# Sparse attention and a mixture of experts on one Trainium2 core: source order in place of scheduled order for the expert part

## The chip, the core and the metric

The kernel runs on one core of one Trainium2 chip. The core has five engines that run their own instruction queues side by side and meet only at semaphores: TensorE for matmuls (PE in the rows, PEld for its weight loads), VectorE (DVE), ScalarE (ACT), GpSimd (POOL) and SyncE, whose queue (SPq) issues the transfers. The metric is the device time of one execution in microseconds, as the median of several runs.

## The reference

Two steps follow each other. The first is block-sparse attention over 4 batches, 8 heads, 768 positions and 64 dimensions per head. The second takes its output as 3072 rows of 512 numbers, gives each row a weight for each of 8 experts by repeated normalisation of rows and columns, and adds up eight two-layer networks:

```python
attn = softmax(where(mask, q @ k.T / sqrt(64), -1e9)) @ v       # [4, 8, 768, 64]
x = attn.transpose(0, 2, 1, 3).reshape(3072, 512)
P = exp(x @ w_gate - max)                                        # [3072, 8]
for _ in range(8):
    P /= P.sum(1) + 1e-9;  P /= P.sum(0) + 1e-9;  P *= 3072 / 8
for e in range(8):
    out += P[:, e:e+1] * (maximum(x @ w1[e], 0) @ w2[e])         # w1[e] 512x1024, w2[e] 1024x512
```

## The kernel before, in words

The attention fills the first 470 us or so and is written out by a table of due times; its instructions are chained one behind the other on each engine, in the order in which they are written. It also brings the first expert's weights in and stores x, split into pieces, in DRAM.

The change is in the expert part that follows. Work goes by `i = 4 e + b`, expert `e` and batch `b` (`B` is 4). Both layers are done by a seven-product scheme on 2x2 blocks: products numbered 0, 1, 5, 6, 3, 4, 2 in the order of use, each of its own combination of blocks. Since every operand is a pair of half-precision numbers (a high and a low part), a product is three matmuls per slice of the contraction.

- **Stage one**, `stage1(i, qi)`: for each of four quarters of half the hidden width, the seven products of x with the first layer's weights. One product is six matmuls of 384 columns into one of four PSUM banks (`p`). Behind each product VectorE folds the bank into the tiles `a1`, `r11`, `u3`, `c21` ("combs", line 1145), ScalarE applies the relu, GpSimd forms the sums that the second stage wants (lines 1207 and 1033). Each of the seven results becomes a pair `h`: a high half on ScalarE (line 1155) and a low half on VectorE or GpSimd (lines 1159 and 1165).
- **Stage two**, `stage2(i, p)`: for product p three groups of twelve matmuls of 256 columns into one of four banks (`py`, line 1248), and behind each group VectorE adds the bank into the output tile `acc` (line 1269).
- **Weights.** The next expert's raw weights come into a single buffer `r` by one transfer of 2 MB (line 173): first `w1`, and once it is used up `w2`. `scale_w` finds their largest number (eight reductions `mx`, line 187, then a few small steps, one of them on TensorE) and from it a power of two. GpSimd forms the differences of blocks that the scheme needs (`queue_sum`, line 1026). Seven splits (`queue_split`) then write the pairs: the high part on ScalarE (line 1011), the low part on VectorE (line 1015). The pairs of w1 lie in the tiles `arena` and `attic` and those of w2 in `w2p`. There is one set of each, so a split has to wait until the old product's last matmul is done.

Four quarters of the next batch alternate with the stage-two products of this one: products 0 and 1, quarter 0, product 5, quarter 1, products 6 and 3, quarter 2, products 4 and 2, quarter 3.

Small steps are put between them by `Slots`, a planner that runs while the kernel is built: each step carries a delay in ticks (one tick per product or group) and costs for VectorE, ScalarE and GpSimd, and it is written into the program when its delay is over and the planner's account of that engine is not ahead of TensorE's. Steps added as `lazy` (weights) come after the urgent ones, in the order in which they were added. What `Slots` writes is the source order. In the kernel before, the framework's own scheduler then orders the instructions of the expert part again on each engine, by a timeline that it estimates itself; only the attention part is chained.

## Time and profile before

| what | value |
|---|---|
| median of 3 runs | 2358.24 us (2353.56 to 2359.13) |
| profiled execution, its own time | 2357.4 us |
| its span | 2355.6 us |
| TensorE busy | 2200.1 us, 93% |
| VectorE busy | 2014.4 us, 86% |
| ScalarE, GpSimd busy | 1256.0 us, 1287.1 us |

The profile is of one execution. Its page gives the busy time of each engine, the span in slices, the chain of work that ended last, and the costliest groups of instructions by source line. The trace behind it can be asked for windows (busy time of each engine in a stretch), for the instructions of a tile or a line, for waits, and for a timeline. A row of a timeline gives start and length in microseconds, engine, line, operation, output and input, and in brackets the idle time before it with what ended that.

### The profile page before, as it was taken

To read this page: it belongs to the slowest core of one execution; us is meant where nothing else is said; L and a number is where in the kernel's file an instruction comes from. 1 tells how busy PE (TensorE), PEld (TensorE's weight loads), DVE (VectorE), ACT (ScalarE), POOL (GpSimd) and SP (SyncE) were. 2 spreads that over 40 slices of the span, in tenths; PEclk is the share of its full clock that TensorE was granted. 3 is DMA by queue.
4 is the path that set the end of the run, shared out by engine and by line. 5 is a ranking of instruction groups with operands and counts; after the bars stand their busy time and mean duration, and the time that the engine had idled before them with its cause. 6 is when DMAs were issued, how large, how long until landed. Compare 5 with 4: busy or idle time off the path is not lost.

```text
span 2355.6 us, 47334 instructions
## 1 busy us (share of the span) xinstructions
PE 2200.1 (93%) x18892; PEld 1608.6 (68%) x18892; DVE 2014.4 (86%) x3570; ACT 1256.0 (53%) x2173; POOL 1287.1 (55%) x1235
## 2 busy tenths in 40 slices
PE   5999998879999999999989999999899999998999
PEld 3766666647666677677667776776677667766777
DVE  8999999888789878987898789878987898789876
ACT  4888878655465445444444445444544454445442
POOL 2012334496367645765576557655865486548543
PEclk9999999999999999999999999999999999999999
DMA  6667765422121212121212121212211221121221
GB/s 152 135 123 151 186 131 121 135 97 75 48 82 50 83 48 83 48 83 48 83 48 83 48 84 52 80 48 83 64 68 48 84 80 52 48 84 48 75 75 54
DMA packets 191888, 192.34 MB, mean 82 GB/s; under 512 B 131740, under 2 KB 144052, under 8 KB 191668
## 3 DMA queue, kind: packets, MB, share of 16 engines
q1 hardware_dynamic: 191104, 189.30, 28.2%
q8 instruction: 147, 2.41, 0.4%
q14 instruction: 73, 0.60, 0.1%
q10 hardware_dynamic: 564, 0.03, 0.0%
HBM read 140.54 MB, written 17.30 MB: 67 GB/s over the span
## 4 chain that ended last, share of the span: by engine, by line
PE 57%; DVE 21%; POOL 9%; issue 6%; DMA 4%; ACT 3%; SPq 0%; DVEq 0%; POOLq 0%; ACTq 0%
PE py L1248 25%; PE p L1135 23%; POOL r L1026 3%; DVE top L673 3%; DMA r<-in_moe_w_dram 3%; DVE h L1165 2%; PE u L731 2%; POOL h L1165 2%; DVE u L1145 2%; DVE acc L1269 2%; DVE mx_w L187 2%; PE t L697 1%; PE m L664 1%; PE t L700 1%; PE m L667 1%
## 5 line engine op out<-in xcount | busy, mean ns | idle before, releaser
L1248 PE MATMUL py<-w2p,h 128*128 128x256 f16 x8064 | 971.1, 275 | 52.7 <-ACT h L1155 23.7
L1248 PEld LDWEIGHTS <-h 128*128 128x128 f16 x8064 | 790.1, 99 | 209.9 <-ACT h L1155 28.8
L1269 DVE SCALAR_TENSOR_TENSOR acc<-py,spare,acc 128x256 f32<-128x256 f32 (+1 forms) x840 | 459.2, 581 | 49.5 <-PE py L1248 46.9
L1165 POOL TENSOR_TENSOR h<-u,h 128x384 f16<-128x384 f32 x128 | 127.0, 992 | 601.3 <-ACT h L1155 601.3
L1135 PEld LDWEIGHTS <-attic 128*128 128x128 f16 x3072 | 301.8, 98 | 195.9 <-issue 22.5
L1135 PE MATMUL p<-attic 128*128 128x384 f16 x2304 | 413.2, 328 | 16.4 <-DVE r L1145 14.4
L1135 PE MATMUL p<-arena 128*128 128x384 f16 x2304 | 407.6, 327 | 19.4 <-DVE a L1145 11.2
L1135 PEld LDWEIGHTS <-arena 128*128 128x128 f16 x2304 | 225.9, 98 | 153.5 <-issue 24.8
L1155 ACT ACTIVATE h<-c 128x384 f16<-128x384 f32 x256 | 133.6, 522 | 330.7 <-DVE c L1145 256.7
L705 ACT ACTIVATE pe<-t,shift,qk 128x768 int32<-128x768 f32 x192 | 189.7, 989 | 78.6 <-PE t L700 73.0
L1145 DVE SCALAR_TENSOR_TENSOR a<-p,a 128x384 f32<-128x384 f32 x384 | 211.1, 550 | 18.9 <-PE p L1135 14.3
L673 DVE TENSOR_REDUCE top<-m 128x1 f32<-128x768 f32 x192 | 181.8, 949 | 16.7 <-PE m L667 16.4
L1155 ACT ACTIVATE h<-r 128x384 f16<-128x384 f32 x256 | 132.5, 521 | 66.5 <-POOL r L1033 63.0
L1207 POOL TENSOR_TENSOR s<-a,u 128x384 f32<-128x384 f32 x128 | 129.6, 1013 | 68.7 <-ACT a L1204 68.7
L1033 POOL TENSOR_TENSOR r<-s,r 128x384 f32<-128x384 f32 x128 | 155.4, 1214 | 9.6
L1033 POOL TENSOR_TENSOR c<-c,r 128x384 f32<-128x384 f32 x128 | 150.8, 1178 | 10.0
L1135 PE MATMUL p<-arena,attic 128*128 128x384 f16 x768 | 146.1, 327 | 0.0
L1026 POOL TENSOR_TENSOR r<-r 128x256 f32<-128x256 f32 (+1 forms) x106 | 135.0, 1290 | 20.0 <-DVE arena L1015 17.9
L664 PE MATMUL m<-kt,qt 128*128 128x512 f16 (+1 forms) x384 | 129.6, 338 | 14.5 <-DVE top L673 7.2
L1165 POOL TENSOR_TENSOR h<-r,h 128x384 f16<-128x384 f32 x128 | 142.8, 1115 | 0.2 <-ACT h L1155 0.2
L1145 DVE SCALAR_TENSOR_TENSOR r<-p,a 128x384 f32<-128x384 f32 x128 | 70.7, 552 | 79.0 <-PE p L1135 59.4
L697 PE MATMUL t<-qt,kt 128*128 128x512 f16 (+1 forms) x384 | 127.9, 333 | 10.8 <-DVE top L673 10.6
(206 smaller groups left out, 3683.1 us busy)
## 6 DMA issues: line engine op xcount, KB each, us to landing
arena<-xd SPq DMA_DIRECT2D x128, 384.0 KB, 3.9
attic<-xd SPq DMA_DIRECT2D x96, 384.0 KB, 3.9
r<-in_moe_w_dram SPq DMA_DIRECT2D x16, 2048.0 KB, 8.4
arena<-in_q_dram SPq DMA_DIRECT2D x16, 384.0 KB, 4.5
arena<-in_k_dram SPq DMA_DIRECT2D x16, 384.0 KB, 4.8
arena<-in_v_dram SPq DMA_DIRECT2D x4, 1536.0 KB, 8.5
xd<-xs_t SPq DMA_DIRECT2D x16, 384.0 KB, 4.6
out_dram<-acc SPq DMA_DIRECT2D x24, 256.0 KB, 2.0
```

Source lines behind the costliest of these rows:

```text
L664: nc.tensor.matmul(sc[:, lo:hi], lhsT=qt[:, 0, c], rhs=ka[:, lo:hi], start=True, stop=False)
L673: nc.vector.tensor_reduce(out=tops[n][:, c : c + 1], in_=sc[:, :S], axis=AX.X, op=ALU.max)
L697: nc.tensor.matmul(sc[:, lo:hi], lhsT=kt[:, 0, c], rhs=qa[:, lo:hi], start=True, stop=False)
L705: nc.scalar.activation(pe, sc[:, :S], AF.Exp, bias=shift, scale=qk[n // 2][3])
L1026: lambda c=c: Pinned.gpsimd.tensor_tensor(out=out[:, c], in0=x[:, c], in1=y[:, c], op=op),
L1033: nc.gpsimd.tensor_tensor(out=out, in0=x, in1=y, op=ALU.subtract)
L1135: nc.tensor.matmul(ps, lhsT=w1p[p][:, l, kc, fs], rhs=xp[p][:, r, kc], start=(kc == 0 and m == 0), stop=(kc == KH - 1 and m == 2),)
L1145: nc.vector.scalar_tensor_tensor(out=t, in0=ps, scalar=HDOWN, in1=other, op0=ALU.mult, op1=ALU.add)
L1155: nc.scalar.activation(h[:, 0], src, AF.Relu if relu else AF.Copy)
L1165: eng.tensor_tensor(out=h[:, 1], in0=src, in1=h[:, 0], op=ALU.subtract)
L1248: nc.tensor.matmul(py, lhsT=hs[i, p, kc][:, l, tsl], rhs=w2p[p][:, r, kc], start=(kc == 0 and m == 0), stop=(kc == KF // 2 - 1 and m == 2),)
L1269: nc.vector.scalar_tensor_tensor(out=dst, in0=src, scalar=c, in1=dst, op0=ALU.mult, op1=ALU.add)
```

## The change

Three things are done at once.

1. Every instruction of the expert part is tied to the one written before it on the same engine (`hold_from(held)` at the end), so that each engine runs in source order. The tie is of a kind that adds no semaphore (`NoSync`): it only binds the scheduler.
2. The splits of the next `w1` are no longer all added at the start of the expert's last batch. They are added inside the last quarter of stage one with the old weights, each behind the old weight's last product (`used`), and taken in another order (6 before 5). `load_w(2, ...)` and `scale_w(2, ...)` stand ahead of quarter 0 and no longer behind it.
3. The differences of `w2` blocks are formed in another way (through `t1`, eight of the sixteen pieces before the scale is known), and its splits come later: 0 and 1 after product 5, 6 and 5 after products 6 and 3, the other three after products 4 and 2.

Some costs and delays of the planner differ too. Only the core of the diff is shown.

```diff
+        def hold_from(n):
+            for ins in traced[n:]:
                 if ins.engine in newest:
                     tc.add_manual_dep(
                         ins, newest[ins.engine], behind, reason="keep_in_program_order"
                     )
                 newest[ins.engine] = ins.name
...
         xlast = finish_x(B - 1)
+        held = len(traced)
...
-            slots.add(part, key, 6 if k == 0 else 1, True, dve=0.6)
+            slots.add(part, key, 8 if k == 0 else 1, True, dve=0.65)
...
-            key, delay, True, act=1.04,
+            key, delay, True, act=1.1,
...
-            key, delay + 1, True, dve=1.2,
+            key, 1, True, dve=1.4,
...
-                key, 1, True, pool=2.4 / n,
+                key, 1, True, pool=3.2 / n,
...
+        def first():
+            one(0, a[0, 0])
+            queue_sum(a[0, 0], a[1, 0], a[0, 0], ("w1", e, 5))
+        def second():
+            one(1, a[0, 1])
+            queue_sum(a[0, 1], a[0, 1], a[0, 0], ("w1", e, 2))
+        def third():
+            one(6, s3)
+            one(5, a[0, 0])
+        return {
+            0: first, 1: second, 6: third,
+            3: lambda: one(3, a[1, 1]), 4: lambda: one(4, a[1, 0]), 2: lambda: one(2, a[0, 1]),
+        }
...
+        def sums():
+            queue_sum(t1, m[0, 1], m[0, 0], ("scale", 2, e))
+            queue_sum(m[0, 1], m[0, 1], m[1, 1], ("scale", 2, e))
+        def first():
+            one(0, m[0, 0])
+            queue_sum(m[0, 0], m[1, 1], t1, ("w2", e, 5))
+            one(1, m[1, 0])
+            queue_sum(m[1, 0], m[1, 0], m[0, 0], ("w2", e, 3))
         return [
-            lambda: one(5, t2),
-            lambda: (one(6, m[0, 1]), one(3, m[1, 0])),
-            lambda: (one(4, m[0, 0]), one(2, m[1, 1])),
+            sums,
+            first,
+            lambda: (one(6, m[0, 1]), one(5, m[0, 0])),
+            lambda: (one(4, t1), one(3, m[1, 0]), one(2, m[1, 1])),
         ]
...
+            if used and p in used:
+                used[p]()
...
-                stage1(i + 1, qi)
+                swap = qi == FH // P - 1 and b == B - 2 and nxt
+                stage1(i + 1, qi, split_w1(e + 1) if swap else None)
...
-        if last:
-            split_w1(e + 1)
         stage2(i, 0)
         stage2(i, 1)
-        quarter(0)
         if last:
...
             load_w(2, e + 1)
-            if not PRE:
-                scale_w(2, e + 1)
+            parts = split_w2(e + 1, wr[2])
+            scale_w(2, e + 1)
+            parts[0]()
             queue_weight(e + 1)
-            parts = split_w2(e + 1, wr[2])
+        quarter(0)
         stage2(i, 5)
         if last:
-            parts[0]()
+            parts[1]()
...
+    hold_from(held)
```

What it moves is best seen in the queues. The names say the batch and the quarter: `p5_15_3` is product 5 of batch 15, quarter 3, and `py_15_1_2` is the third group of stage-two product 1. Batch 15 is the last of expert 3, so the weights that change here are those of expert 4. Lines from 1017 on stand a little lower in the changed file: 1015 has become 1021, 1145 has become 1165, 1165 has become 1185, 1269 has become 1289, 1011 has become 1017.

VectorE before, in the last quarter with expert 3's weights:

```order
L1145 SCALAR_TENSOR_TENSOR r11_15_3_18694<-p1_15_3_18695,a1_15_3_18685 128x384
L1015 SCALAR_TENSOR_TENSOR arena_92<-r1_4_17448,sw1_4_17452,arena_92 128x1024
L1145 SCALAR_TENSOR_TENSOR a1_15_3_18685<-p5_15_3_18706,a1_15_3_18685 128x384
L1015 SCALAR_TENSOR_TENSOR attic_96<-s3_4_17454,sw1_4_17452,attic_96 128x1024
L1145 SCALAR_TENSOR_TENSOR u3_15_3_18714<-p6_15_3_18715,a1_15_3_18685 128x384
L1165 TENSOR_TENSOR h_5_8094<-r11_15_3_18694,h_5_8094 128x384
L1015 SCALAR_TENSOR_TENSOR attic_96<-r1_4_17448,sw1_4_17452,attic_96 128x1024
L1145 SCALAR_TENSOR_TENSOR c21_15_3_18723<-p3_15_3_18724,u3_15_3_18714 128x384
L1015 SCALAR_TENSOR_TENSOR arena_92<-r1_4_17448,sw1_4_17452,arena_92 128x1024
L1015 SCALAR_TENSOR_TENSOR attic_96<-r1_4_17448,sw1_4_17452,attic_96 128x1024
L1145 SCALAR_TENSOR_TENSOR u3_15_3_18714<-p4_15_3_18734,u3_15_3_18714 128x384
```

The same place now, and then the end of the stage-two products 0 and 1 behind it:

```order
L1021 SCALAR_TENSOR_TENSOR arena_92<-r1_4_17448,sw1_4_17452,arena_92 128x1024
L1165 SCALAR_TENSOR_TENSOR r11_15_3_18698<-p1_15_3_18699,a1_15_3_18685 128x384
L1185 TENSOR_TENSOR h_5_8094<-r11_15_3_18698,h_5_8094 128x384
L1021 SCALAR_TENSOR_TENSOR arena_92<-r1_4_17448,sw1_4_17452,arena_92 128x1024
L1165 SCALAR_TENSOR_TENSOR a1_15_3_18685<-p5_15_3_18712,a1_15_3_18685 128x384
L1165 SCALAR_TENSOR_TENSOR u3_15_3_18721<-p6_15_3_18722,a1_15_3_18685 128x384
L1021 SCALAR_TENSOR_TENSOR attic_96<-s3_4_17454,sw1_4_17452,attic_96 128x1024
L1165 SCALAR_TENSOR_TENSOR c21_15_3_18734<-p3_15_3_18735,u3_15_3_18721 128x384
L1165 SCALAR_TENSOR_TENSOR u3_15_3_18721<-p4_15_3_18744,u3_15_3_18721 128x384
```

```order
L1185 TENSOR_TENSOR h_25_8114<-a1_15_3_18685,h_25_8114 128x384
L1021 SCALAR_TENSOR_TENSOR arena_92<-r1_4_17448,sw1_4_17452,arena_92 128x1024
L1289 SCALAR_TENSOR_TENSOR acc_3_10006<-py_15_1_2_18862,spare_6_16716,acc_3_10006 128x256
L1021 SCALAR_TENSOR_TENSOR attic_96<-r1_4_17448,sw1_4_17452,attic_96 128x1024 x3
L1165 SCALAR_TENSOR_TENSOR r11_16_0_18897<-p1_16_0_18898,a1_16_0_18888 128x384
L1165 SCALAR_TENSOR_TENSOR a1_16_0_18888<-p5_16_0_18908,a1_16_0_18888 128x384
```

Before, all seven splits stand within that one quarter, ahead of its last combs; now three stand in the quarter and four behind the stage-two groups that follow it. The low half `h_5`, which needs ScalarE's answer to the comb of `r11`, had two combs and two splits between it and that comb; now it comes right behind.

VectorE before, at the splits of w2:

```order
L1015 SCALAR_TENSOR_TENSOR w2p_0_8082<-r2_4_18957,sw2_4_18961,w2p_0_8082 128x1024
L1269 SCALAR_TENSOR_TENSOR acc_3_10006<-py_15_2_2_19374,spare_6_16608,acc_3_10006 128x256
L1015 SCALAR_TENSOR_TENSOR w2p_1_8083<-r2_4_18957,sw2_4_18961,w2p_1_8083 128x1024
L1165 TENSOR_TENSOR h_25_8114<-s1_16_2_19266,h_25_8114 128x384
L1165 TENSOR_TENSOR h_20_8109<-a1_16_2_19190,h_20_8109 128x384
L1015 SCALAR_TENSOR_TENSOR w2p_2_8084<-r2_4_18957,sw2_4_18961,w2p_2_8084 128x1024
L1145 SCALAR_TENSOR_TENSOR r11_16_3_19400<-p1_16_3_19401,a1_16_3_19390 128x384
L1145 SCALAR_TENSOR_TENSOR a1_16_3_19390<-p5_16_3_19414,a1_16_3_19390 128x384
L1015 SCALAR_TENSOR_TENSOR w2p_4_8086<-r2_4_18957,sw2_4_18961,w2p_4_8086 128x1024
```

VectorE now:

```order
L1021 SCALAR_TENSOR_TENSOR w2p_0_8082<-r2_4_18881,sw2_4_18886,w2p_0_8082 128x1024
L1165 SCALAR_TENSOR_TENSOR a1_16_3_19379<-p5_16_3_19410,a1_16_3_19379 128x384
L1165 SCALAR_TENSOR_TENSOR u3_16_3_19419<-p6_16_3_19420,a1_16_3_19379 128x384
L1165 SCALAR_TENSOR_TENSOR c21_16_3_19430<-p3_16_3_19431,u3_16_3_19419 128x384
L1179 SCALAR_TENSOR_TENSOR h_19_8108<-c21_16_3_19430,h_19_8108 128x384
L1021 SCALAR_TENSOR_TENSOR w2p_1_8083<-r2_4_18881,sw2_4_18886,w2p_1_8083 128x1024
L1165 SCALAR_TENSOR_TENSOR u3_16_3_19419<-p4_16_3_19444,u3_16_3_19419 128x384
```

Four splits within nine rows have become two within seven; the other five now come after stage-two product 1 of batch 16 and later.

ScalarE at the start of the expert part, before (batch 0, quarter 1):

```order
L1155 ACTIVATE h_4_8093<-a1_0_0_8121 128x384
L769 ACTIVATE xf_3_6824<-u_0_144 128x384
L1011 ACTIVATE w2p_0_8082<-r2_0_7728,sw2_0_7732 128x1024
L1011 ACTIVATE w2p_1_8083<-r2_0_7728,sw2_0_7732 128x1024
L1011 ACTIVATE w2p_2_8084<-r2_0_7728,sw2_0_7732 128x1024
L1155 ACTIVATE h_7_8096<-r11_0_1_8209 128x384
```

And now (batch 0, the end of quarter 3):

```order
L1224 ACTIVATE a1_0_3_8362<-a1_0_3_8362 128x384
L1017 ACTIVATE w2p_0_8082<-r2_0_7728,sw2_0_7732 128x1024
L1286 ACTIVATE acc_0_8119<-py_0_0_0_8465 128x512 x2
L1286 ACTIVATE acc_0_8119<-py_0_0_1_8480 128x512 x2
L1286 ACTIVATE acc_0_8119<-py_0_0_2_8495 128x512 x2
L1017 ACTIVATE w2p_1_8083<-r2_0_7728,sw2_0_7732 128x1024
```

The first expert's w2 splits have moved from the second quarter of the first batch to behind its last. On TensorE the first product of the expert part now stands behind the attention's last matmul, and no group of matmuls is cut up by another any more.

36 lines of the change are left out of this document (11 added, 25 removed).

## The prediction

> **What bounds the kernel now.** I read the page first, then windows one expert long, then the moments in which TensorE waits.
>
> ```profile
> span 2355.6 us, 47334 instructions
> PE 2200.1 (93%) x18892; PEld 1608.6 (68%) x18892; DVE 2014.4 (86%) x3570; ACT 1256.0 (53%) x2173; POOL 1287.1 (55%) x1235
> ```
>
> Two engines are near full. In the chain of waits (start, length, what) the load of each expert's w2 marks a period, and the long pieces give TensorE's own pace:
>
> ```profile
> 699.22 9.23 DMA r<-in_moe_w_dram
> 931.79 8.52 DMA r<-in_moe_w_dram
> 1361.32 7.32 PE py L1248 x67
> 1368.63 3.90 PE p L1135 x24
> 2101.10 8.50 DMA r<-in_moe_w_dram
> ```
>
> Five periods take 2101.10 - 931.79, so one takes 233.9 us. Unhindered, a product of stage one is 3.90/4 = 0.975 and a stage-two group 12 x 7.32/67 = 1.31. An expert has 4 x 4 x 7 products (109.2) and 4 x 7 x 3 groups (110.1): 219.3 us. So 14.6 us of each period are lost. The windows of one period (length; busy time of PE, PEld, DVE, ACT, POOL; clock) say where:
>
> ```profile
> 931.80:1165.80 234.00, 224.26 (x1682) 164.95 (x1682) 199.00 (x344) 110.03 (x206) 145.43 (x137) 0.99 0.20 66
> 1145.00:1185.00 40.00, 35.18 (x267) 25.53 (x265) 35.12 (x53) 17.02 (x27) 18.89 (x16) 1.00 0.39 122
> 1210.00:1240.00 30.00, 24.27 (x169) 16.27 (x167) 27.78 (x35) 15.67 (x26) 29.61 (x28) 0.96 0.36 115
> 1240.00:1385.00 145.00, 144.47 (x1106) 108.35 (x1105) 116.57 (x215) 65.59 (x130) 84.20 (x82) 1.00 0.14 49
> ```
>
> For 145 us TensorE never stops, with VectorE at 80%. It stops where the weights change: at w1's splits (1145 to 1185) and at w2's (1210 to 1240), with VectorE at 88 and 93% and GpSimd full in the second. Its waits there, and VectorE's queue:
>
> ```profile
> 1164.65 1.14 PE L1135 MATMUL p<-arena 128*128 128x384 f16 x6 [1.66 <-DVE a L1145]
> 1237.93 3.53 PE L1248 MATMUL py<-w2p,h 128*128 128x256 f16 x17 [3.21 <-ACT h L1155]
> 1158.52 2.28 DVE L1015 SCALAR_TENSOR_TENSOR attic<-r,sw,attic 128x1024 f16<-128x1024 f32 x1
> 1161.19 1.27 DVE L1015 SCALAR_TENSOR_TENSOR arena<-r,sw,arena 128x1024 f16<-128x1024 f32 x1
> 1163.58 0.55 DVE L1145 SCALAR_TENSOR_TENSOR u<-p,u 128x384 f32<-128x384 f32 x1
> 1164.05 0.54 DVE L1145 SCALAR_TENSOR_TENSOR a<-p,a 128x384 f32<-128x384 f32 x1
> 1165.71 2.72 DVE L1269 SCALAR_TENSOR_TENSOR acc<-py,spare,acc 128x512 f32<-128x512 f32 x4
> 1170.59 1.26 DVE L1269 SCALAR_TENSOR_TENSOR acc<-py,spare,acc 128x256 f32<-128x256 f32 x3
> ```
>
> A split takes 1.27 to 2.28; the combs that free the banks queue behind seven of them.
>
> **The change, part by part.** It adds no work: seven splits, eight reductions and the sums stay. What counts is when VectorE gets them. A comb costs 0.47 (1163.58 to 1164.05), a wide acc 0.67, a narrow one 0.41. The rest come from the groups (busy, mean ns), less 0.08 which overlaps with the next:
>
> ```profile
> L1165 DVE TENSOR_TENSOR h<-a,h 128x384 f16<-128x384 f32 x128 | 127.4, 995 | 0.3 <-ACT h L1155 0.3
> L1165 DVE TENSOR_TENSOR h<-s,h 128x384 f16<-128x384 f32 x128 | 106.8, 834 | 27.3 <-ACT h L1155 27.1
> L1165 DVE TENSOR_TENSOR h<-r,h 128x384 f16<-128x384 f32 x128 | 97.3, 760 | 15.0 <-ACT h L1155 14.8
> L1159 DVE SCALAR_TENSOR_TENSOR h<-c,h 128x384 f16<-128x384 f32 x128 | 78.6, 614 | 2.4 <-ACT h L1155 2.4
> L187 DVE TENSOR_REDUCE mx_w<-r 128x1 f32<-128x512 f32 x128 | 79.1, 673 | 16.1 <-DMA r<-in_moe_w_dram 16.1
> L1015 DVE SCALAR_TENSOR_TENSOR attic<-r,sw,attic 128x1024 f16<-128x1024 f32 x21 | 33.8, 1608 | 0.0
> ```
>
> So low halves 0.91, 0.75, 0.68, 0.53, a reduction 0.59, a split 1.53. A quarter is 7 combs and two low halves: 4.5 against TensorE's 6.8. Counting the new queue piece by piece at the change of expert (VectorE against TensorE): the last old quarter with three splits, one of them ahead of its first comb, 9.1 against 6.8, less 1.5 done while the groups before it (which leave 2.7 free) run: +0.8; product 0, +0.1; product 1 with four splits and two low halves 9.0 against 3.9: +5.1. VectorE is then 6.0 behind. TensorE has four banks, so it runs three products (2.9) ahead: **3.1 us lost** at the new quarter 0. Then the spare time of quarters (2.3 each) pays the rest off; the eight reductions add 4.8 over quarter 1 and three products, and leave VectorE under 1 behind. A second hump stands at the next batch: two splits in quarter 3 (+1.1), two behind product 1 (+2.1), one each in quarter 0 (-0.8) and behind product 5 (+2.4): 4.8, **1.9 us lost**. I take 5 per change of expert. Bounds: nothing lost (0), and as now (14.6).
>
> Covered: the load of w2 is issued behind the last split, lands 8.5 later, and its first reduction stands 6.8 + 3.9 + 3.9 = 14.6 behind; if it came late, VectorE would stop and every comb behind it. SyncE has the seven x loads ahead of it, as now. The regrouped differences are sixteen pieces as before, eight of them ahead of the scale. With quarters 13.7 apart on average and GpSimd at 145.4/16 = 9.1 per quarter, they find room. The ties cost nothing by themselves; the price is that an engine no longer steps around a wait.
>
> That price falls due at the **start**, where the scheduler had mixed attention, batch 0, the last x pieces and w2's splits:
>
> ```profile
> 462.20:572.80 110.60, 95.36 (x744) 65.50 (x742) 94.06 (x153) 59.18 (x113) 81.77 (x73) 0.97 0.23 80
> 463.40 0.55 DVE L716 TENSOR_SCALAR pl<-pe 128x768 f16<-128x768 uint16 x1
> 475.97 3.22 ACT L1011 ACTIVATE w2p<-r,sw 128x1024 f16<-128x1024 f32 x3
> 501.73 2.08 PE L1135 MATMUL p<-arena 128*128 128x384 f16 x6 [5.72 <-DVE c L1145]
> 504.03 2.12 PE L1135 MATMUL p<-arena 128*128 128x384 f16 x6
> ```
>
> In 110.6 us eight quarters and 21 groups were done (82.1), so some 25 were lost, after the attention's rest. Now the first product waits for the attention's last weights (463.40) and what hangs on them: about 467 instead of 462.2, 4.5 later. The splits of w2, which ScalarE did at 476, come behind quarter 3, one by one between the copies of the output: following the queue with 1.07 (3.22 for three) for a high half and 1.27 to 1.53 for a low one I get waits of about 6.6, 3.6 and 7.3 ahead of products 0, 1 and 5. The last x pieces, now within product 2, cost about 7 in two waits for splits, and small waits 5. That is 30 lost plus 4.5, against 25: +10. After waits this long matmuls run at half pace for a while (2.08 and 2.12 for six, where 1.14 is usual): two such waits for one, +2. I take **+12**; bounds -20 (all lost time goes, but the later start stays) and +30 (the x pieces' chain costs twice, the balance steps stop TensorE too).
>
> Sum: 2355.6 - 7 x (14.6 - 5) + 12 = 2300.4 of span. The profiled execution took 2357.4, 1.8 more than its span, and the median is 0.8 above it: **2303 us**.
>
> **Rivals.** *Splits at the slow price.* Now w1's first splits stand next to GpSimd's sums, and by order the last three wait on ScalarE behind halves that GpSimd's chain feeds. At 2.28 each (1158.52) seven splits put 5.3 more on VectorE, 10 lost instead of 5: 2303 + 35 = 2338. Against it: 1.27 occurs as well. The Trainium skill (SBUF — State Buffer, Who interferes with whom) says that a VectorE instruction with two SBUF inputs shuts out, or is shut out by, a GpSimd one that reads SBUF. The trace agrees: combs, with one input there, stay at 0.55, splits spread. By that rule alone, always losing, it would be this rival.
>
> *All of it goes.* TensorE never stops at a change and the start costs what it did: 2358 - 102 = 2256. For it: 145 us without a stop. Against: 6.0 behind is more than four banks cover.
>
> *VectorE becomes the bound.* In order, it stops where the low half of r11 comes right behind its comb. What that takes stands here:
>
> ```profile
> 1198.88 0.56 DVE L1145 SCALAR_TENSOR_TENSOR r<-p,a 128x384 f32<-128x384 f32 x1 [0.25 <-ACT a L1180]
> 1199.98 0.51 ACT L1184 ACTIVATE r<-r 128x384 f32<-128x384 f32 x1
> 1200.52 0.52 ACT L1155 ACTIVATE h<-r 128x384 f16<-128x384 f32 x1
> ```
>
> From 1199.44 to 1201.04: 1.6, and some 0.6 for c21. VectorE's 199.0 per period plus 16 quarters x 2.2 is 234: the point from which it is slower. At 2.5 a quarter it is 239 for each of eight experts: 2358 + 8 x 5.1 + 12 = 2411. Against it: the low half comes right behind only where the planner counts VectorE as free, and in the 145 us it has 28 to spare, 2.7 a quarter. The Trainium skill (TensorE: Matmul & The Clock Gate, Architectural detail) calls VectorE's and ScalarE's queues strict FIFO, which is what makes such a stop total; it changes none of these numbers.
>
> *Nothing to see.* The same work on a VectorE as full as before: the waits only move, and the start eats the rest: 2358.
>
> **Chances.** Forecast 0.55, slow splits 0.18, all of it 0.14, VectorE bound 0.09, nothing 0.04. A difference under 0.3% can't be told from none. Faster: 0.55 + 0.18 + 0.14 = 0.87; same 0.04; slower 0.09. The range runs from between "all of it" and the forecast to "slow splits": 2266 to 2340; 0.04 + 0.09 and about half of 0.14 lie outside.
>
> **What would show it.** Right: period near 224, the windows at w1's and w2's splits at 95% for TensorE, three splits within the last old quarter, TensorE's longest waits of a period at new quarter 0 for DVE r; w2's load issued about 22 after the last old quarter begins; waits over 5 us only between 495 and 570. Wrong: waits for combs in batches without weight work (VectorE bound), a first reduction that waits for the DMA, a period over 229 with splits near 2.2, or an expert part that reaches the second w2 load (699.22 now) much earlier or later than 711 less 5 to 10.

## The result and the profile after

The changed kernel takes **2467.7 us** (median of 4 runs, 2458.15 to 2477.5) where the kernel before takes 2357.37 beside it: a ratio of 1.0471, 95% interval 1.0427 to 1.0514. It is slower by 110 us; 2303 was forecast. The profile after is of the fastest of the four executions (2458.15), so it accounts for 100.8 of the 110 us. In the text below "lead" is the distance that TensorE can run ahead of VectorE because four PSUM banks hold its products, and a "stop" is time in which an engine stands in front of an instruction whose input isn't there.

The head of the page after:

```profile
span 2456.4 us, 47436 instructions
PE 2206.7 (90%) x18892; PEld 1611.4 (66%) x18892; DVE 1995.6 (81%) x3570; ACT 1270.8 (52%) x2173; POOL 1255.0 (51%) x1235
```

The work is the same, and the busy times hardly differ (TensorE 2200.1 then, 2206.7 now; VectorE 2014.4 then, 1995.6 now). Of the 100.8 us of span, 94 are idle time of TensorE. The issues of SyncE's weight loads say where (start, length; w2 of experts 1, 2 and 7):

```profile
743.74 0.38 SPq L173 DMA_DIRECT2D r<-in_moe_w_dram  x1
...
989.78 0.38 SPq L173 DMA_DIRECT2D r<-in_moe_w_dram  x1
...
2203.53 0.38 SPq L173 DMA_DIRECT2D r<-in_moe_w_dram  x1
```

The first mark is 44.5 later than before (699.22). The last five periods take (2203.53 - 989.78)/5 = 242.8 instead of 233.9, and the one ahead of them 246.0 instead of 232.6: 57.9 in all. Behind the last mark 1.6 are won. So there are two losses: about 44 at the start and about 9 in each period of 243.

One period in windows (length; busy time of PE, PEld, DVE, ACT, POOL; clock): the whole, the stretch behind the w2 load, the clear middle, and the last old quarter with what follows it up to the next load:

```profile
1476.10:1718.40 242.30, 222.13 (x1682) 164.14 (x1682) 197.12 (x344) 111.83 (x206) 141.12 (x136) 1.00 0.19 64
1476.10:1561.50 85.40, 74.25 (x561) 54.63 (x561) 75.19 (x127) 41.13 (x74) 53.16 (x53) 1.00 0.18 58
1561.50:1694.20 132.70, 129.56 (x990) 96.59 (x989) 100.19 (x190) 57.42 (x114) 74.46 (x73) 1.00 0.17 59
1694.20:1718.40 24.20, 18.32 (x135) 12.92 (x133) 21.74 (x28) 13.27 (x19) 13.50 (x11) 1.00 0.34 114
```

TensorE idles for 20.2 of 242.3: 11.2 behind the load, 3.1 in the middle, 5.9 in the last old quarter. So 17 of 20 are still lost where the weights change, in 110 us. VectorE works 96.9 of these 110.

What is new is VectorE's own idle time. Its longest waits over the whole run (engine, line and tile, what ended them: us in all, times, longest), first after, then the row of before that answers to the first (c21's halves, at L1159 then, had 2.4):

```profile
DVE h L1185 <- ACT h L1175: 172.0, 174, 1.2
...
DVE h L1179 <- ACT h L1175: 53.6, 91, 0.6
```

```profile
DVE h L1165 <- ACT h L1155: 42.3, 104, 1.9
```

VectorE stands in front of low halves, waiting for ScalarE's high halves, for 225.6 us. At r11's it waits about 1.1 in 93 of the 128 quarters, those in which the half stands right behind its comb, and at c21's 0.6 in 91. The remaining 61 us are at s1's halves, which had 27 before. The waits at r11 and c21 are the stop of the third rival. TensorE's waits after:

```profile
PE p L1153 <- DVE a L1165: 54.0, 44, 2.7
PE p L1153 <- DVE r L1165: 43.4, 28, 3.1
PE all_w L110 <- DVE ma_w L193: 23.6, 14, 2.9
```

The third is new as well: in order, TensorE stands in front of the transpose that spreads a weight's maximum until VectorE has reduced it.

VectorE's queue and TensorE's at the last old quarter (start, length, instruction, in brackets the idle time ahead of it):

```profile
1695.20 1.28 DVE L1021 SCALAR_TENSOR_TENSOR arena<-r,sw,arena 128x1024 f16<-128x1024 f32 x1 [2.05 <-ACT arena L1017]
1696.40 0.55 DVE L1165 SCALAR_TENSOR_TENSOR r<-p,a 128x384 f32<-128x384 f32 x1
1698.09 1.38 DVE L1185 TENSOR_TENSOR h<-r,h 128x384 f16<-128x384 f32 x1 [1.15 <-ACT h L1175]
1699.40 1.27 DVE L1021 SCALAR_TENSOR_TENSOR arena<-r,sw,arena 128x1024 f16<-128x1024 f32 x1
1700.59 0.55 DVE L1165 SCALAR_TENSOR_TENSOR a<-p,a 128x384 f32<-128x384 f32 x1
```

```profile
1701.19 1.14 PE L1153 MATMUL p<-attic 128*128 128x384 f16 x6 [2.72 <-DVE a L1165]
1714.38 0.82 PE L1153 MATMUL p<-arena 128*128 128x384 f16 x4 [1.91 <-DVE arena L1021]
```

A split stands ahead of the first comb and waits 2.05 for ScalarE; then the low half waits 1.15; then the next split; and the comb of product 5, which would free a bank, ends at 1701.14. TensorE waits 2.72 for it.

### The profile page after: what moved, and what is told of

Read it like the earlier page. It is cut to its first block, busy times and chain, and to the rows that moved or that the text cites. A ratio compares the mean times of both kernels' runs of the same rounds, so it can differ in the third digit from the quotient of the medians.

```text
span 2456.4 us, 47436 instructions
## 1 busy us (share of the span) xinstructions
PE 2206.7 (90%) x18892; PEld 1611.4 (66%) x18892; DVE 1995.6 (81%) x3570; ACT 1270.8 (52%) x2173; POOL 1255.0 (51%) x1235
## 4 chain that ended last, share of the span: by engine, by line
PE 53%; DVE 32%; ACT 6%; issue 5%; DMA 2%; POOL 1%; SPq 0%; DVEq 0%; POOLq 0%
PE py L1268 26%; PE p L1153 20%; DVE acc L1289 5%; DVE h L1185 4%; DVE a L1165 3%; DVE top L673 3%; DVE w2p L1021 3%; ACT h L1175 2%; DVE u L1165 2%; PE u L731 2%; DVE mx_w L187 2%; DVE r L1165 1%; PE m L664 1%; PE t L697 1%; PE m L667 1%
## 5 line engine op out<-in xcount | busy, mean ns | idle before, releaser
L1268 PE MATMUL py<-w2p,h 128*128 128x256 f16 x8064 | 917.9, 275 | 27.9 <-ACT w2p L1017 14.2
L1185 POOL TENSOR_TENSOR h<-u,h 128x384 f16<-128x384 f32 x128 | 131.9, 1030 | 766.0 <-ACT h L1175 766.0
L1289 DVE SCALAR_TENSOR_TENSOR acc<-py,spare,acc 128x256 f32<-128x256 f32 (+1 forms) x840 | 447.2, 581 | 19.1 <-PE py L1268 11.5
L1153 PE MATMUL p<-arena 128*128 128x384 f16 x2304 | 400.7, 328 | 9.4 <-DVE arena L1021 7.4
L1185 DVE TENSOR_TENSOR h<-r,h 128x384 f16<-128x384 f32 x128 | 87.3, 682 | 111.0 <-ACT h L1175 110.8
L1185 DVE TENSOR_TENSOR h<-s,h 128x384 f16<-128x384 f32 x128 | 118.1, 923 | 60.9 <-ACT h L1175 60.8
L1204 ACT ACTIVATE r<-r 128x384 f32<-128x384 f32 x128 | 66.9, 523 | 188.3 <-DVE r L1165 188.3
L1039 POOL TENSOR_TENSOR c<-c,r 128x384 f32<-128x384 f32 x128 | 142.8, 1115 | 28.0 <-ACT c L1232 18.1
L1039 POOL TENSOR_TENSOR r<-s,r 128x384 f32<-128x384 f32 x128 | 146.5, 1145 | 10.0
L1185 POOL TENSOR_TENSOR h<-r,h 128x384 f16<-128x384 f32 x128 | 138.3, 1081 | 4.8 <-ACT h L1175 4.8
L1032 POOL TENSOR_TENSOR r<-r 128x256 f32<-128x256 f32 (+1 forms) x106 | 122.5, 1181 | 28.6 <-DVE arena L1021 28.6
```

The costliest lines, as they stand in the source:

```text
L1032: lambda c=c: Pinned.gpsimd.tensor_tensor(out=out[:, c], in0=x[:, c], in1=y[:, c], op=op),
L1039: nc.gpsimd.tensor_tensor(out=out, in0=x, in1=y, op=ALU.subtract)
L1153: nc.tensor.matmul(ps, lhsT=w1p[p][:, l, kc, fs], rhs=xp[p][:, r, kc], start=(kc == 0 and m == 0), stop=(kc == KH - 1 and m == 2),)
L1185: eng.tensor_tensor(out=h[:, 1], in0=src, in1=h[:, 0], op=ALU.subtract)
L1268: nc.tensor.matmul(py, lhsT=hs[i, p, kc][:, l, tsl], rhs=w2p[p][:, r, kc], start=(kc == 0 and m == 0), stop=(kc == KF // 2 - 1 and m == 2),)
L1289: nc.vector.scalar_tensor_tensor(out=dst, in0=src, scalar=c, in1=dst, op0=ALU.mult, op1=ALU.add)
```

## The experiments

All times are medians beside the kernel before on the same chip, which gave 2354.7 to 2359. A period is a fifth of the time between the w2 loads of experts 2 and 7 in the profiled execution; for the changed kernel it is 242.8, for the kernel before 233.9.

### The order, the places, the start and the low halves

**The order alone**, on the kernel before:

```diff
         xlast = finish_x(B - 1)
+        held = len(traced)
...
             load_x(i + 2)
+    hold_from(held)
```

> The kernel before with one thing added: from the first expert on every engine runs in source order. Splits, differences and planner costs stay as before. Theory (the order costs the time: VectorE stops on ScalarE's answer behind the comb of r11, and the start is no longer mixed): slower than before by at least as much as the change, 2440 to 2500, period 240 or more, VectorE's waits of low half L1165 on ScalarE near 170 us in all (42.3 before). Rival (the new places of the splits and the regrouped differences cost it, the order is free): within 15 of 2357, period 234.

Measured: 2607.12, ratio 1.1064 (1.1037 to 1.1092), period 264.6, slower than the 2440 to 2500 expected. VectorE waits 214.2 at the low halves of r11, a1 and s1 (170 expected). Order alone costs 249 us. The new places of the splits, the regrouped differences and the planner's costs together are therefore worth 140 us to a program in source order; they were not taken apart. In this kernel one period reads:

```profile
1829.10:2093.20 264.10, 230.86 (x1682) 165.75 (x1682) 196.30 (x343) 111.59 (x206) 141.25 (x136) 0.94 0.17 59
```

The same matmuls keep TensorE busy 8.7 longer than in the changed kernel (222.13), at a clock of 0.94 against 1.00: with more waiting, what runs between the waits is slower too.

**The places without the order**, the changed kernel with its ties taken out:

```diff
-    hold_from(held)
```

> The changed kernel without its ties: new places of the splits, regrouped differences and new planner costs stay, and the scheduler orders the expert part again. Theory (order costs the time): near the kernel before, 2330 to 2365, period 230 to 235, first w2 mark near 699. Rival (the places of the splits and the differences cost it): near 2467, period 243. If the scheduler undoes the places of the splits altogether, it is 2357 with a period of 234.

Measured: 2360.35, ratio 1.0006 (0.9992 to 1.0021), period 235.0, first mark 697.2. Where the scheduler sets the order, the places and the regrouping make no difference that can be told. All that is lost is lost through the order.

**The first expert left to the scheduler:**

```diff
             finish_late()
+        if i == B:
+            for ins in traced[held:]:
+                newest[ins.engine] = ins.name
+            held = len(traced)
```

> The changed kernel with the scheduler free for the first expert's four batches, and source order from the second expert on. Theory: the 44.5 us by which the first w2 mark comes later than before belong to the order at the start, so the mark is back near 700 to 710 and the time near 2425 to 2435; the later periods stay at 243. Rival (the mark comes late through steady stops in the quarters of the first expert, as in every other): the free first expert also gains, with the same sum; the split between the two is read from the first 110 us (start) against the rest of the first expert. Rival (ties further on cost something at the seam): 2467 or above.

Measured: 2414.7, ratio 1.0240 (1.0215 to 1.0265). The first mark:

```profile
692.13 0.38 SPq L173 DMA_DIRECT2D r<-in_moe_w_dram  x1
```

It is 51.6 earlier than in the changed kernel, and the time is 53 less, more than the 44.5 by which the mark had come late; the later periods are 244.4. So nearly half of the loss belongs to the first expert.

**Low halves two ticks later**, so that they no longer stand right behind the comb:

```diff
-                slots.add(low, key, delay + 1, dve=0.47)
+                slots.add(low, key, delay + (1 if delay else 3), dve=0.47)
```

> The changed kernel with the low halves of r11, c21 (and u3) made due two ticks later, so that they don't stand right behind the comb whose ScalarE answer they need; the work is the same. Theory: VectorE's wait for ScalarE at low halves falls from 21.5 and 6.5 us per period to under 8, and the period from 243 to 225 to 234: 2360 to 2415, the late start staying. Rival (VectorE isn't what bounds the period, its stops are idle time that TensorE leaves it): the waits go, the period stays at 241 to 244, 2455 to 2470. Rival (the delayed halves bring stage two's products late): slower than 2467.

Measured: 2455.52, ratio 1.0414 (1.0388 to 1.0441), period 242.8. By the medians that is 12 less than the changed kernel, with intervals that touch. The stops are gone (1.9 us per period left at L1185, none at L1179), and the period of the profiled execution is what it was, so the theory of the time, that they cost the 9 us per period, falls, and the numbers are those of the first rival. What they did cost shows between the changes. The nine quarters from the end of the w2 splits to the last old quarter hold w1's reductions but no splits. Start to start, with the same matmuls, first in the changed kernel, then here:

```profile
1563.90:1692.50 128.60, 125.46 (x958) 93.41 (x957) 98.31 (x187) 55.39 (x110) 70.61 (x70) 1.00 0.17 60
```

```profile
1568.30:1692.70 124.40, 124.40 (x957) 93.37 (x956) 95.67 (x183) 55.48 (x108) 71.29 (x68) 1.00 0.18 63
```

They became 4.2 shorter, and the rest of the period longer by as much. Two things are seen there. VectorE still stands: in the stretches that answer to the 110 us above it waits 10.2 for ScalarE, where it was 9.6. Its waits on ScalarE's halves of the splits in one period, and the split that answers to the one at 1699.40 above:

```profile
DVE arena L1021 <- ACT arena L1017: 4.2, 2, 2.2
DVE w2p L1021 <- ACT w2p L1017: 4.2, 3, 1.6
```

```profile
1695.47 1.28 DVE L1021 SCALAR_TENSOR_TENSOR arena<-r,sw,arena 128x1024 f16<-128x1024 f32 x1 [2.05 <-ACT arena L1017]
...
1699.41 1.28 DVE L1021 SCALAR_TENSOR_TENSOR arena<-r,sw,arena 128x1024 f16<-128x1024 f32 x1 [2.19 <-ACT arena L1017]
```

The second split starts 3.94 behind the first; in the changed kernel it was 4.20. The low half has left its place, and the split, now next in line, waits for the same engine for nearly as long. Here the stop has only moved.

The second is pace. TensorE's waits fell by 4.3 in the period (from 20.2 to 15.9), but it was busy 227.14 instead of 222.13 for as many matmuls. The granted clock was 0.94 behind the load and 0.93 in the last old quarter, against 1.00 in the changed kernel. A place where that shows, first the changed kernel and then this one:

```profile
1551.05 1.14 PE L1153 MATMUL p<-attic 128*128 128x384 f16 x6 [1.18 <-ACT a L1200]
1554.12 2.11 PE L1153 MATMUL p<-attic 128*128 128x384 f16 x12 [1.94 <-DVE r L1165]
```

```profile
1553.23 1.14 PE L1153 MATMUL p<-attic 128*128 128x384 f16 x6 [2.06 <-ACT a L1200]
1555.78 4.00 PE L1153 MATMUL p<-attic 128*128 128x384 f16 x12 [1.41 <-DVE r L1165]
```

Behind waits of 2.06 and 1.41 twelve matmuls take 4.00; behind 1.18 and 1.94 they take 2.11. What the period would be at an equal clock is not shown.

**Both gains together**, the free first expert and the late low halves, by the two edits above:

> The two edits that gained, together: the first expert free for the scheduler, and the low halves two ticks later. If they are independent, 53 and 12 add up: 2395 to 2408. If the late halves gained only at the start (there VectorE stood in front of ScalarE in four quarters in a row), nothing is left of the 12: 2410 to 2420.

Measured: 2403.04, ratio 1.0190 (1.0173 to 1.0207), period 242.3. The sum holds; here the late halves shorten the period (244.4 to 242.3). This is the fastest version that does all of the work in source order from the second expert on; it does not reach the kernel before.

### Is it VectorE, and which single stop?

**Thin splits:** the low halves of the weights on 64 of 1024 columns.

```diff
+        n = 64
...
+                out=dst[:, 1][:, :1, :n], in0=src[:, :1, :n], scalar=s, in1=dst[:, 0][:, :1, :n],
+                op0=ALU.mult, op1=ALU.subtract,
+            ) if key[1] else Pinned.vector.scalar_tensor_tensor(
...
```

> The changed kernel, with the low halves of the weight splits computed on 64 of 1024 columns from the second expert on (the rest of those halves keeps older values): about 14 x 1.3 = 18 us less VectorE work per change of expert, every order and every wait as in the changed kernel. Theory now (the earlier one fell with the late low halves; the period is set where the weights change, and there by VectorE's queue, work and stops together): the period falls from 243 to 224 to 232, 2380 to 2415. Rival (TensorE waits there for ScalarE's high halves or for the order itself, VectorE's work is not the limit): period 238 to 243, 2445 to 2467.

Measured: 2384.69, ratio 1.0127 (1.0109 to 1.0144), period 230.7.

```profile
1441.00:1671.90 230.90, 223.26 (x1684) 164.89 (x1683) 181.83 (x343) 111.81 (x206) 136.41 (x136) 0.99 0.20 67
```

15.3 us less on VectorE (197.12 to 181.83), all of it where weights change, shorten the period by 12.1, although its stops in front of low halves are all still there (172.9 us at r11's, a1's and s1's, 53.6 at c21's). VectorE's work at the change sets most of what a period loses.

**Three repairs**, each of one stop seen in the trace: the first w1 splits' low halves two ticks later; the transpose that spreads the maximum four ticks later; the load of w2, ahead of which four splits are forced out in a row, behind the new quarter 0.

```diff
-            key, 1, True, dve=1.4,
+            key, 1, True, dve=1.4, gap=2 if key[0] == "w1" and key[2] in (0, 1, 6) else 0,
```

> The changed kernel, with the low halves of w1's first three splits held back two ticks more, so that VectorE does not stand in front of ScalarE's high half (2.05 us at 1695.20, a comb queued behind it). Theory (that stop costs TensorE its 2.72 us wait in the last old quarter): VectorE's wait for arena from ScalarE goes from 14.2 in all to under 4, 1.5 to 2.5 per change, 2450 to 2457. Rival (what is held back piles up ahead of the load of w2, five splits in a row instead of four): no gain, 2464 to 2485, with a longer wait at the new quarter 0.

```diff
-        slots.add(spread, key, 1, True, gap=2)
+        slots.add(spread, key, 1, True, gap=6)
```

> The changed kernel, with the transpose that spreads a weight's maximum placed four ticks later, so that TensorE does not stand in its own queue until VectorE has reduced (2.59 us at 1502.83, 23.6 in all). Theory (TensorE is in order too, and this stop is lost time): about 1.5 per scale, 14 scales: 2440 to 2455. Rival (VectorE is behind anyway and catches up meanwhile): 2460 to 2470, the same time waited for combs instead.

```diff
         stage2(i, 1)
+        quarter(0)
         if last:
...
             queue_weight(e + 1)
-        quarter(0)
         stage2(i, 5)
```

> The changed kernel, with the four last splits of w1 no longer forced out in one go ahead of the load of w2: the load and the queueing of w2's work stand behind the new quarter 0 instead of ahead of it, and each split then comes at the latest ahead of its own product. Theory (four splits in a row, 5.6 us on VectorE, hold up the first combs of the new quarter: TensorE waits 1.91 and 1.67 there): both waits go, w2's work starts 7 us later without harm: 2 to 4 per change, 2440 to 2455. Rival (w2's splits then come too late for the next batch's stage two): slower than 2467, waits of py for w2p in every period.

Measured: 2500.88 (1.0622, 1.0599 to 1.0646), 2491.86 (1.0583, 1.0567 to 1.0599) and 2491.83 (1.0576, 1.0553 to 1.0598), periods 247.6, 246.7 and 245.7. The first two remove their stop, the third shrinks its wait (1.91 has become 0.24), and each is slower. TensorE's waits from 900 to 2250, one row of each kernel in that order:

```profile
PE py L1268 <- ACT w2p L1017: 30.3, 5, 6.1
```

```profile
PE py L1268 <- ACT w2p L1017: 29.3, 5, 5.9
```

```profile
PE p L1153 <- DVE attic L1021: 25.2, 12, 2.3
```

The lazy queue hands out load, reductions, spread and splits in one line. Only its front item can go, so what holds that back delays everything behind it. In the first two the second split of w2 comes late, and stage-two product 1 waits 6 us for it in every change; in the third two w1 splits are late for their products (2.3 and 1.7). There is no slack in that line to be handed round.

**One engine freed, or one alone held:**

```diff
-        def hold_from(n):
+        def hold_from(n, only=None):
             for ins in traced[n:]:
+                if only and not only(ins.engine):
+                    continue
...
-    hold_from(held)
+    hold_from(held, lambda g: g != nc.vector.engine)
```

and in the same way "only VectorE held" and "all but ScalarE held".

> The changed kernel with VectorE's instructions left to the scheduler; TensorE, ScalarE, GpSimd and SyncE keep source order. Theory (the loss is VectorE's fixed queue: it can't put a comb ahead of a split or of a half that waits): most of the loss goes, 2350 to 2385, period 232 to 236. Rival (TensorE's own fixed order, its stops at the spread maximum and at the start's stage two included, costs as much): 2400 to 2450.

> The changed kernel with VectorE alone in source order, the other four engines left to the scheduler. Theory: VectorE's order alone carries most of the loss, 2430 to 2470, period 240 or more. Rival (it takes the order of TensorE or ScalarE as well): 2355 to 2410.

> The changed kernel with ScalarE left to the scheduler, the others in source order. Theory: ScalarE is busy half of the time and its order decides little: 2440 to 2470. Rival (VectorE's stops come from ScalarE serving its queue in the wrong order): 2380 to 2430.

Measured: 2451.64 (1.0402, 1.0384 to 1.0420), 2442.02 (1.0360, 1.0344 to 1.0375), 2483.16 (1.0532, 1.0517 to 1.0548); periods 245.1, 240.3, 245.7. VectorE's order alone does most of the damage (85 us), as expected. But freeing VectorE alone mends almost nothing, which was not: the first mark comes 15 earlier, and the periods are longer. Freeing ScalarE alone costs another 15 us, where 2440 to 2470 was expected; the cause was not looked into. The theory that VectorE's queue is at fault by its order falls in that form: with the other engines held, the scheduler finds not much better an order for a free VectorE. Read with the kernel without ties, what it gains it gains by ordering the engines together; through which of their waits was not taken apart.

### Where VectorE has room

Added work on VectorE, the same 10 low halves of r11 more per expert, put in different quarters:

```diff
+                more_work = p == 0 and i >= B and (i % B, qi) in (...)
+
+                def lows():
+                    for _ in range(3 if more_work else 1):
+                        low()
+
-                slots.add(low, key, delay + 1, dve=0.47)
+                slots.add(lows, key, delay + 1, dve=0.47)
```

> The changed kernel, from the second expert on, with the low half of r11 computed three times instead of once in five quarters of each expert that hold no weight work (third batch, and the first quarter of the fourth): 5 x 2 x 0.5 = 5 us more VectorE work per expert, same order. Theory (VectorE bounds only the stretch in which the weights change): TensorE's lead covers it, 0 to 1.5 per expert, 2467 to 2478. Rival (VectorE with its stops bounds the whole period, as the prediction's third rival had it): 4 to 5 per expert, 2495 to 2507.

> The same 5 us of VectorE work per expert, but in the first five quarters after the new w1 comes into use (first batch, and the first quarter of the second). Theory: nearly all of it is lost, 4 to 5.5 per change, 2490 to 2506. Rival (the loss there comes from TensorE's own waits, not from VectorE's queue): under 2 per change, 2467 to 2480.

> The same added VectorE work as in e14_busy_mid, moved to the five quarters between w1's last reduction and w1's first split (third quarter of the third batch to the third quarter of the fourth). In e14 two of the five quarters held w1's eight reductions (1640.40 to 1654.13), and 7 of the 8.8 us lost per expert lie there. Theory (VectorE with its stops is the bound wherever weight work is queued, and not elsewhere): 0 to 2.5 per expert, 2467 to 2485. Rival (VectorE bounds everywhere): 5 to 9 per expert as before, 2500 to 2530.

Measured: 2529.76 (1.0731, 1.0712 to 1.0750), 2519.41 (1.0686, 1.0669 to 1.0702) and 2515.69 (1.0663, 1.0641 to 1.0684); periods 252.1, 250.3, 251.0. VectorE's busy time per period rose by 7.3, 6.1 and 7.4, and the period by 9.3, 7.5 and 8.2: as much or more is lost, wherever it is put, and the first two times lie above all that was expected. The theory that VectorE bounds only the change of weights, and is free in between, falls. (The quarters of the first of the three were badly chosen: two held w1's reductions. The third run mends that, with the same outcome.)

It is not lost evenly. In the third run, three of the five quarters take only 0.35 longer for 1.2 us of added work, with waits of 0.18. Most is lost in two: in one the added halves take 4.14 and TensorE waits 2.58, in the other it waits 2.22. More goes in slower matmuls behind waits: that period is 9.6 longer than the changed kernel's above, with 2.4 more waits and 7.2 more busy time of TensorE, at a clock of 0.97.

This stood against the late low halves, which took 26 of 28 us of stops out of a period and left it as long as it was. A way to have both: in every clear quarter the stops use up most of the lead without exceeding it, so that they cost little themselves, and what is added finds too little left. Then the added work must become free once the stops are gone, outside the change. Both placements, on top of the late low halves:

> e4_late_low (the stops of the low halves gone) with the added VectorE work of e17_busy_clear (7.4 us of VectorE busy time per expert, which cost 7.7 there). Theory (the two stops of a quarter, 1.15 and 0.59, and the halves behind them use up the lead that four banks give TensorE, so that nothing more fits; without the stops there is room): the added work costs 0 to 2 per expert, 2455 to 2470. Rival (VectorE's work alone fills the period, stops or not): 5 to 8 per expert, 2490 to 2515.

> e4_late_low with the added VectorE work of e15_busy_change (6 us busy per expert, which cost 7.0 there), in the quarters after the weights change. Theory (there splits and reductions fill VectorE even without the stops): 4 to 7 per expert, 2485 to 2505. Rival (without the stops there is room here too): 0 to 2 per expert, 2455 to 2470.

Measured: **2459.68** (1.0437, 1.0421 to 1.0452) and **2513.52** (1.0661, 1.0643 to 1.0679), against 2455.52 without the added work, the second a little above what was expected; periods 242.4 and 250.4 against 242.8. One period of each:

```profile
1476.10:1718.40 242.30, 226.70 (x1684) 165.68 (x1683) 201.36 (x354) 112.51 (x206) 144.06 (x136) 0.98 0.19 64
```

```profile
1503.00:1754.30 251.30, 231.04 (x1684) 167.23 (x1683) 203.14 (x354) 111.92 (x206) 142.88 (x136) 0.96 0.18 62
```

In the clear quarters 7.2 more busy time (194.15 to 201.36) cost nothing; where the weights change 9.0 more (to 203.14) cost 7.6. The nine clear quarters with the added work, first with the stops, then without them:

```profile
1600.60:1736.70 136.10, 128.01 (x958) 94.07 (x957) 104.19 (x193) 54.87 (x108) 68.66 (x68) 0.99 0.17 57
```

```profile
1566.50:1691.20 124.70, 124.70 (x959) 93.51 (x957) 102.09 (x193) 54.96 (x108) 71.78 (x68) 1.00 0.18 62
```

With the stops the work costs 7.5 there (128.6 to 136.1), without them 0.3 (124.4 to 124.7). That separates the two: in the changed kernel the stops take most of the lead in the clear quarters, and at the change added work is lost with or without them.

## Why the prediction was wrong, step by step

**What bounds the kernel.** That TensorE's time is lost at the change of weights, behind VectorE, was right, and it is still so after (17 of 20.2 us per period).

**The step that failed** is the count at the change of expert, "I take 5 per change of expert". 242.8 - 219.3 = 23.5 are lost, 17.0 of them as TensorE's waits at the change; the rest are the 3.1 in the middle and some 3 by which the matmuls take longer than the unhindered 219.3. The first term of the count, "**3.1 us lost** at the new quarter 0", came out: 1.91 (shown above) and 1.67:

```profile
1718.82 2.11 PE L1153 MATMUL p<-attic 128*128 128x384 f16 x12 [1.67 <-DVE r L1165]
```

The rest of the walk did not:

```profile
1502.83 0.32 PE L110 MATMUL all_w<-ident,ma_w 128*128 128x128 f32 x1 [2.59 <-DVE ma_w L193]
...
1523.31 1.14 PE L1153 MATMUL p<-attic 128*128 128x384 f16 x6 [2.01 <-DVE a L1165]
...
1539.93 2.11 PE L1153 MATMUL p<-attic 128*128 128x384 f16 x12 [1.77 <-DVE r L1165]
```

In the last old quarter, where it had no wait, TensorE waits 2.7. In quarter 2, where VectorE was to be "under 1 behind", it waits 3.0, most of it for the transpose. At the second hump, from quarter 3 to quarter 1 of the next batch, where **1.9 us lost** was said, it waits 7.7 (2.01, 0.79, 1.77, 1.18 and 1.94).

The walk laid VectorE's instructions end to end, each at its busy time, as if none waited. The places are the ones foreseen (three splits in the last old quarter, one ahead of its first comb, four ahead of the new quarter 0, two each in quarter 3 and behind product 1), and splits were not dearer than taken. But in order, VectorE also stands: in the 110 us of a change 2.0 for arena, 4.8 at the low halves of line 1185, 1.8 at c21's and 1.0 elsewhere, 9.6 on ScalarE in all. With 96.9 of work that is 106.5 of 109.6, and of the rest 1.6 is waiting for TensorE: VectorE has next to no gap left there. That its work counts there is shown by the thin splits (15.3 less work, 12.1 less time). That the 9.6 of waits count in the same way is argued: no run took them away. The lead of 2.9 us, for its part, is no reserve between the changes either: the stops take most of it in every clear quarter, as the runs with added work show.

A second omission is TensorE's own queue. The transpose behind the reductions stops it for 23.6 us in all, 3.1 in the period shown; the sum had no term for it. The prediction said that the price of the ties "is that an engine no longer steps around a wait", and then counted this price, in its sum, at the start alone. Moving the transpose did not win this time back, as the second repair showed.

**The start**, +12, was 44.5 at the first mark. Its walk was right where it went. TensorE's waits ahead of stage-two products 0, 1 and 5, and the first of those for the x pieces:

```profile
503.19 0.37 PE L1268 MATMUL py<-w2p,h 128*128 128x256 f16 x1 [5.13 <-ACT w2p L1017]
505.02 5.44 PE L1268 MATMUL py<-w2p,h 128*128 128x256 f16 x35 [1.46 <-DVE w2p L1021]
512.67 0.27 PE L1268 MATMUL py<-w2p,h 128*128 128x256 f16 x1 [2.21 <-ACT w2p L1017]
514.17 5.65 PE L1268 MATMUL py<-w2p,h 128*128 128x256 f16 x35 [1.24 <-DVE w2p L1021]
533.55 0.37 PE L1268 MATMUL py<-w2p,h 128*128 128x256 f16 x1 [6.90 <-ACT w2p L1017]
535.86 5.38 PE L1268 MATMUL py<-w2p,h 128*128 128x256 f16 x35 [1.94 <-DVE w2p L1021]
...
574.44 0.19 PE L369 MATMUL lg<-gh,xs_b 128*128 128x8 f16 x1 [4.99 <-DVE xs_b L355]
```

6.6, 3.45 and 8.8 where 6.6, 3.6 and 7.3 were said; the x pieces 7.5 where 7 was said. What it left out is the rest of the first expert. Of the four quarters at the head, with no groups between them, the last three make TensorE wait for combs; one of these waits:

```profile
487.08 1.14 PE L1153 MATMUL p<-attic 128*128 128x384 f16 x6 [1.71 <-DVE a L1165]
```

Such waits come to 6.6 us up to 497; the balance steps took 9.0 where 5 was said for small waits, and the window from 461.5 to 573.3 ran at a clock of 0.91, against 0.97 in the stretch quoted of before. That the order in the first expert is the cause is shown by leaving it free (53 us). How it divides can be read from windows: from the first product to the first mark it is 282.2 us where it was 237.0; TensorE idles 55.0 of them where it idled 22.9, and is busy 227.2 where it was 214.1. So some 32 are waits and 13 busy time, at a clock of 0.91 up to 573 and 0.93 behind it; the prediction had 2 for slower matmuls. (The window before also holds the last of the attention, which now comes ahead of it.) The first product did not come 4.5 later but at 461.5, 0.7 earlier.

**The rivals.** *Slow splits*: did not happen; a split takes 1.41 on average (75 splits, 105.5 us from 900 to 2200) against 1.63 before. *All of it goes* and *Nothing to see* fell with the sign. *VectorE becomes the bound* had the mechanism, the row and the sign, at a chance of 0.09, and was priced at 2411. Its threshold was wrong. By its own count the stops would have had to reach 2.2 per quarter; they are 28.0/16 = 1.75 with s1's halves counted in, under the break-even, and the kernel is still slower. An average over the period doesn't decide: at the change VectorE has next to no spare time, while in the clear quarters it has some and the stops cost 4.2. The reason given against it ("the low half comes right behind only where the planner counts VectorE as free") failed outright: the planner emits it right behind in 93 of 128 quarters, since by its count VectorE *is* free. It counts work; it does not count that the half waits for ScalarE.

**What would show it** was well named: "waits for combs in batches without weight work" stood under the signs of a wrong forecast, and there are some, though small (0.73 at 1668.95, none after the stops are taken out). So was the first mark, at 743.74 where 711 less 5 to 10 was said.

**The chances** put 0.87 on faster. The trace held a warning that was given 0.09: the scheduler's order hid a known stop of 1.6 us per quarter, and it was about to go. With that order back, and all else as in the changed kernel, VectorE's waits at line 1185 are 57.1 in place of 172.0.

## What to carry to other kernels

Where a program is put in source order, walk each engine's queue with its waits on other engines, not with busy times alone; a half that needs another engine's answer and stands right behind its question was a stop of nearly fixed length here, whether or not the engine had time to spare. Spend a buffer lead once: where each repetition already uses most of it, little can be added, and a removed stop only shows where the next instruction in line does not wait for the same answer. Read TensorE's busy time beside its waits: here 4 us won in one stretch went with slower matmuls in another. Stretches in which several phases run mixed, such as the start, are where a free order is worth most: here half of the loss came from one expert of eight.

## What the hardware showed that was not expected

Repeating a low half three times (the run with added work in the clear quarters) took 1.74 us in most quarters, and 4.14 in one quarter of each of experts 1 to 6. VectorE there, and GpSimd beside it:

```profile
1662.74 4.14 DVE L1185 TENSOR_TENSOR h<-r,h 128x384 f16<-128x384 f32 x3 [1.15 <-ACT h L1175]
...
1681.84 1.74 DVE L1185 TENSOR_TENSOR h<-r,h 128x384 f16<-128x384 f32 x3 [1.14 <-ACT h L1175]
```

```profile
1663.35 3.11 POOL L1032 TENSOR_TENSOR r<-r 128x512 f32<-128x512 f32 x2
...
1677.81 0.90 POOL L1185 TENSOR_TENSOR h<-c,h 128x384 f16<-128x384 f32 x1
```

While GpSimd makes the sums of w1, each half takes 1.4 instead of 0.6; at 1681.84 GpSimd had nothing to do. In the last expert, which has no next w1 and so no such sums, the same quarter took 1.74. The Trainium skill (SBUF — State Buffer, Who interferes with whom) says that a VectorE instruction with two SBUF inputs contends with a GpSimd one that reads SBUF; this trace agrees, with a factor of 2.4.

TensorE's pace fell after waits that were each short: 2.06 and 1.41 with six matmuls between them, then twelve matmuls in 4.00 instead of 2.11, at a granted clock of 0.72 from 1550 to 1562 (1.00 at that place of the changed kernel). The Trainium skill (TensorE: Matmul & The Clock Gate, Part 1: The HAM clock gate (the "warmup" mystery)) puts the half rate behind at least one idle window of about 3.4 us; here no single wait was that long, and the two come to 3.47. That the two waits count together is read from this place alone; no run tested it.
